# Another written-out order of a fused linear-attention and feed-forward kernel

## The chip, the cores and the metric

The kernel runs on one core of one Trainium2 chip. The metric is the device time of one execution, in microseconds, as the median over runs; lower is better. The core has five engines that each work through their own list of instructions in order: PE (matmul), DVE and ACT (elementwise work), POOL (elementwise work and the issue of DMAs that convert a type on the way) and SP (the issue of other DMAs). They wait for each other by semaphores alone. Matmul results land in PSUM, eight banks of 128 x 512 f32, which DVE and ACT read and POOL does not in this kernel.

## What is computed

```python
def phi(x):                       # q and k scaled by 64 ** -0.25 first
    proj = einsum('bhsd,md->bhsm', x, omega)
    h = proj - sum(x * x, -1) / 2
    return exp(h - max(h, -1)) / sqrt(m)
kv  = einsum('bhsm,bhsd->bhmd', phi(k), v)
z   = sum(phi(k), over s)
num = einsum('bhsm,bhmd->bhsd', phi(q), kv)
den = einsum('bhsm,bhm->bhs', phi(q), z) + 1e-6
x   = (num / den) as 4608 rows of 512      # 8 batches x 576 tokens, 8 heads x 64
h   = x @ w_in                             # 512 x 2048
out = (h * clip(h + 3, 0, 6) / 6) @ w_out  # 2048 x 512
```

All inputs and the output are f32.

## The kernel before

The program first lists its 1963 operations and then emits them. An operation is one call of `op(...)`; it has a number (its place in the listing), a name, the engines that may take it, what it reads and writes, and a function that emits its instructions. The table `ORDER` at the top holds, for each engine, the numbers of the operations in the order in which that engine runs them. `Prog.schedule` walks these lists: the list in which a number stands is the engine that does the operation, and nothing is ever moved past its neighbour. `Prog.emit` then puts a semaphore wait ahead of an instruction where a predecessor runs on another engine. So an instruction that must wait holds up everything behind it in its list. 76 small dummy matmuls ("idle", L576) may be put where the schedule leaves PE empty in the first 21 us; the trace shows 65 of them.

**Stage 1, attention of one batch** (`attention`, `pair`, `burst`; b = 0 to 7). DMAs load k, q and v (`load`, L622): for batch 0 in f32, for later ones k and q through POOL's queue in bf16, and v through SP's. Each of these has main parts (names like v00, v10, k00, k10, q01: 512 tokens of each head) and a leftover (kl, ql0, ql1, vl: the last 64 tokens). k and q are transposed: on PE for batches 0 and 1 (names T), by transposing DMAs on SP after that (Tdmak, Tdmaq, L748). K and Q are matmuls with omega; from batch 3 on both go in four bursts R (L767, L770). ACT takes the exponentials eK and eQ (L786, L795, L818, L835). DVE takes the maxima mx and their reciprocals cc. v is scaled by cc into vc (L939, on POOL in one instruction or on ACT in eight), vcc is its column of cc, vcl the same for leftovers. kv (L957, L959) is the product over tokens, kvz its copy out of PSUM, num (L985) the product with the q side, rec and div the division by the denominator. The result x goes through X, Xdma and Sdma (transposes) to xT, or to xS for the leftover tokens of all batches, which make up a ninth block. The buffer v32 exists once, vl, vc and vcl twice.

**Stage 2, feed-forward of one block of 512 tokens** (`mlp`; block 0 to 8, one block behind the attention). mm1 (L1054; L1199 for block 0, whose weights arrive in four quarters wi0 to wi3, L595, wi0 in two halves) gives the hidden units, relu on ACT and g on DVE (L1060, L1062, L1208, L1210) the activation, in f16. The second product goes by seven block products P.0 to P.6 (L1312) of sums and differences of quarter matrices, a scheme with seven products in place of eight; the sums S1 to S4 of the activations run on POOL (L1240), and on POOL or DVE for the later half of block 8. Results leave PSUM as p1, u2, u3, C11, C21, C22, C12 (L523, L1328) into the one buffer osb, and then by the stores outw (L1408). Block 0 uses a plain product instead, mm2 (L1224), with stores out.0.0 to out.0.3 (L1234). Blocks 7 and 8 use seven products for the first matmul too (`mm1_pair`, mm1a to mm1d, L1133; copies s1, s2, s3; sums a1, a2). The last product of block 8 goes in three parts, P8.60 to P8.62 (L1381), with stores outl (L1392).

**What sets the order around the places that matter below.** w_in's quarters wait for the landing of q11.0 (`W_GATE`) and go through POOL's queue, in POOL's list order. PE's op 431, mm1.0A.12, is the first that needs wi3. vl and v of batch b = 2 wait for a piece of w_out; for b from 3 on they wait for the mm1 of block b - 2 with at = 9, which for vl.3 is mm1.1.12. v00.2 also waits until the vc of batch 1 have read v32. In block 8, P8.3 adds into the PSUM bank that u2.8 reads first.

| numbers | names | engines allowed |
|---|---|---|
| 33, 34, 35, 36, 37 | wi0 (two halves), wi1, wi2, wi3 | POOL |
| 17, 19, 22 to 25, 31, 32 | k00, k01, q00, q10, q01, q11, ql0, ql1 of batch 0 | SP |
| 120, 123, 132, 126, 135, 129, 141 | castk0.10, castk0.11, castq0.0B, .0A, .1B, .1A, .l | POOL, ACT, DVE by part |
| 192, 193, 195, 210, 225, 226, 240, 241 | vcl.0 twice, vc.0.0, vc.0.1, vc.0.2, vcc.0.2, vc.0.3, vcc.0.3 | POOL, ACT |
| 197, 199, 212, 431 | kv.0.0, num.0.0A, kv.0.1, mm1.0A.12 | PE |
| 468, 469, 470, 690 | vl.2, v00.2, v10.2, vl.3 | SP |
| 402, 584, 614 | Sdma.1, out.0.0, out.0.3 | SP |
| 635, 683, 684, 685 | S31.0 (S3 of block 1), k00.3, k10.3, kl.3 | POOL |
| 523, 524, 526, 528 | vcl.2 twice, vc.2.0, kv.2.0 | 528 PE, others POOL or ACT |
| 796, 797 | u2.1, P1.3 | DVE, PE |
| 1806, 1895, 1924 | X2.8, S18.2, S18.3 (S1 of block 8) | POOL, DVE |
| 1921, 1922, 1923, 1799, 1803, 1937 | g1.8.7, S38.3, S28.3, C21.7, C12.7, u2.8 | DVE |
| 1893, 1894, 1931 to 1934 | S38.2, S28.2, S48.0 to S48.3 | POOL, DVE |

Of the kernel before, what the change touches and what calls it, by code (L numbers as in the profile page):

```python
# [20 lines left out]
        13, 118, 139, 156, 124, 144, 150, 162, 115, 168, 147, 127, 153, 121, 159, 165, 136, 130, 133, 177, 185, 175,  # L21
        183, 197, 187, 142, 212, 179, 181, 199, 204, 214, 171, 227, 242, 202, 217, 229, 244, 219, 410, 416, 173, 189,
        417, 232, 404, 254, 247, 405, 222, 234, 406, 207, 249, 407, 257, 411, 412, 418, 413, 419, 422, 280, 425, 252,
        237, 260, 428, 300, 431, 434, 437, 440, 286, 284, 282, 443, 318, 306, 303, 288, 446, 449, 309, 312, 452, 298,
        296, 455, 315, 324, 294, 345, 458, 290, 575, 292, 321, 353, 576, 577, 327, 341, 335, 585, 586, 337, 339, 587,
        595, 588, 596, 331, 605, 366, 333, 578, 329, 579, 597, 355, 589, 590, 379, 598, 591, 368, 371, 592, 392, 580,
        581, 343, 606, 599, 381, 358, 607, 384, 600, 582, 394, 397, 601, 374, 608, 361, 609, 602, 387, 400, 610, 611,
        612, 638, 514, 626, 506, 629, 512, 623, 641, 632, 653, 504, 508, 499, 647, 644, 662, 656, 659, 484, 475, 487,
        496, 478, 481, 674, 668, 520, 518, 490, 493, 677, 510, 516, 671, 784, 785, 528, 502, 794, 533, 540, 530, 787,
        545, 542, 800, 564, 552, 788, 717, 554, 795, 569, 566, 557, 797, 798, 697, 801, 803, 804, 710, 807, 808, 811,  # L30
        817, 826, 724, 820, 737, 814, 832, 841, 829, 835, 739, 742, 749, 844, 847, 850, 761, 862, 856, 859, 773, 754,
        865, 778, 766, 751, 972, 988, 775, 973, 763, 982, 975, 976, 983, 885, 985, 986, 989, 898, 991, 992, 1005, 999,
        1014, 1002, 995, 996, 1017, 905, 1008, 1023, 1020, 1029, 925, 1035, 1032, 912, 1038, 1044, 937, 1050, 927,
        1047, 949, 1053, 939, 942, 930, 1160, 1161, 1176, 954, 961, 1170, 966, 951, 963, 1163, 1171, 1086, 1164, 1173,
        1174, 1073, 1177, 1179, 1180, 1093, 1202, 1193, 1190, 1187, 1183, 1184, 1100, 1205, 1196, 1113, 1208, 1217,
        1211, 1118, 1220, 1223, 1125, 1226, 1115, 1137, 1127, 1235, 1130, 1139, 1238, 1232, 1142, 1149, 1241, 1348,
        1349, 1151, 1364, 1154, 1351, 1274, 1352, 1358, 1359, 1281, 1365, 1361, 1362, 1390, 1375, 1378, 1381, 1367,
        1368, 1393, 1371, 1372, 1384, 1405, 1261, 1399, 1414, 1396, 1420, 1411, 1408, 1426, 1301, 1313, 1429, 1303,
        1318, 1306, 1536, 1315, 1423, 1325, 1537, 1288, 1552, 1539, 1540, 1327, 1546, 1330, 1547, 1462, 1337, 1549,
        1342, 1339, 1550, 1553, 1469, 1555, 1556, 1476, 1559, 1560, 1449, 1563, 1569, 1566, 1572, 1581, 1501, 1593,  # L40
        1506, 1503, 1489, 1584, 1525, 1494, 1578, 1491, 1530, 1527, 1513, 1587, 1518, 1596, 1515, 1599, 1602, 1614,
        1608, 1611, 1617, 1631, 1632, 1662, 1675, 1634, 1665, 1691, 1678, 1667, 1635, 1680, 1704, 1670, 1694, 1641,
        1720, 1696, 1683, 1642, 1707, 1699, 1723, 1709, 1733, 1644, 1645, 1725, 1712, 1749, 1736, 1650, 1738, 1728,
        1762, 1752, 1651, 1741, 1754, 1809, 1765, 1647, 1648, 1812, 1767, 1822, 1757, 1654, 1814, 1655, 1770, 1825,
        1817, 1838, 1827, 1778, 1779, 1841, 1851, 1830, 1843, 1867, 1781, 1854, 1782, 1846, 1856, 1880, 1870, 1788,
        1872, 1859, 1883, 1789, 1885, 1909, 1875, 1794, 1896, 1791, 1792, 1888, 1899, 1795, 1912, 1901, 1941, 1914,
        1797, 1798, 1904, 1917, 1801, 1935, 1925, 1926, 1802, 1936, 1928, 1929, 1938, 1939, 1942, 1960, 1957, 1945,
# [3 lines left out]
        0, 21, 17, 23, 19, 22, 25, 24, 31, 27, 32, 26, 28, 29, 30, 269, 270, 271, 474, 473, 472, 471, 470, 468, 690,  # L51
        469, 402, 614, 584, 694, 696, 594, 693, 695, 692, 604, 536, 548, 560, 572, 691, 573, 881, 878, 810, 883, 879,
        806, 745, 757, 781, 769, 882, 782, 880, 884, 1069, 998, 1072, 1066, 1070, 1071, 994, 1068, 933, 945, 970, 957,
        969, 1067, 1260, 1259, 1257, 1258, 1186, 1133, 1121, 1145, 1157, 1182, 1254, 1158, 1256, 1255, 1374, 1370,
        1447, 1445, 1446, 1448, 1309, 1443, 1333, 1321, 1345, 1444, 1346, 1442, 1509, 1497, 1533, 1521, 1562, 1558,
        1534, 1653, 1657, 1800, 1804, 1953, 1952, 1959, 1962, 1950, 1956,
    ],
    "ACT": [
        18, 20, 117, 119, 157, 145, 151, 163, 132, 169, 148, 129, 154, 193, 166, 196, 160, 178, 211, 184, 137, 176,
        186, 225, 182, 180, 243, 188, 172, 218, 174, 190, 223, 408, 414, 420, 423, 281, 426, 238, 208, 429, 253, 432,  # L60
        301, 435, 438, 441, 283, 285, 444, 261, 319, 307, 304, 447, 310, 450, 313, 289, 299, 352, 297, 325, 346, 316,
        453, 291, 293, 354, 322, 328, 342, 336, 338, 456, 340, 332, 378, 367, 334, 391, 330, 459, 390, 380, 344, 593,
        583, 362, 375, 388, 401, 613, 507, 515, 630, 627, 624, 513, 642, 633, 639, 654, 505, 509, 500, 648, 645, 603,
        663, 657, 660, 476, 497, 482, 479, 485, 675, 488, 494, 519, 669, 491, 523, 511, 672, 517, 503, 529, 539, 678,
        521, 551, 550, 553, 565, 720, 718, 723, 722, 706, 703, 704, 700, 708, 698, 403, 713, 711, 716, 715, 736, 709,
        812, 702, 748, 818, 747, 729, 821, 727, 815, 725, 730, 827, 833, 830, 836, 759, 842, 848, 845, 851, 863, 857,
        774, 860, 866, 974, 977, 897, 894, 891, 896, 892, 888, 886, 899, 890, 903, 921, 901, 1000, 1006, 1003, 923,
        1015, 1018, 906, 936, 904, 1009, 1024, 908, 1021, 911, 1030, 910, 1036, 1033, 913, 574, 915, 1039, 1045, 918,
        938, 1051, 1048, 917, 1054, 959, 960, 962, 1091, 1087, 1092, 1089, 1079, 1084, 1076, 1082, 1074, 1078, 1080,
        1085, 1098, 1099, 1094, 1096, 1194, 1191, 1108, 1203, 1188, 1112, 1111, 1206, 1103, 1197, 1105, 1101, 1209,  # L70
        1212, 1124, 1136, 1218, 1221, 1106, 1224, 1126, 1227, 1138, 1147, 1148, 1239, 1233, 1236, 1242, 1350, 1277,
        1280, 1279, 1275, 1284, 1287, 1282, 1376, 1353, 1379, 1391, 1382, 1286, 1312, 1394, 1385, 1406, 1262, 1270,
        1268, 1266, 1400, 1264, 1415, 1267, 1397, 1297, 1412, 1273, 1409, 1272, 1427, 1324, 1421, 1323, 1430, 1538,
        1424, 1293, 1291, 1289, 1541, 1336, 1294, 1338, 1468, 1465, 1463, 1467, 1474, 1472, 1470, 1159, 1475, 1479,
        1477, 1482, 1481, 1450, 1452, 1458, 1456, 1564, 1455, 1570, 1567, 1454, 1488, 1573, 1502, 1461, 1582, 1460,
        1490, 1585, 1526, 1579, 1514, 1594, 1588, 1597, 1603, 1600, 1609, 1615, 1612, 1618, 1633, 1663, 1664, 1676,
        1677, 1666, 1692, 1679, 1671, 1693, 1636, 1673, 1695, 1684, 1705, 1706, 1686, 1722, 1708, 1700, 1724, 1702,
        1713, 1734, 1735, 1715, 1750, 1737, 1729, 1731, 1753, 1763, 1742, 1764, 1744, 1758, 1810, 1813, 1823, 1760,
        1771, 1824, 1773, 1826, 1818, 1820, 1839, 1831, 1842, 1780, 1852, 1853, 1847, 1833, 1783, 1849, 1860, 1881,
        1882, 1862, 1884, 1876, 1878, 1897, 1889, 1891, 1900, 1913, 1905, 1918, 1907, 1920, 1927, 1930, 1948, 1949,  # L80
        1951,
    ],
    "DVE": [
        16, 12, 11, 15, 14, 5, 138, 4, 9, 140, 10, 125, 7, 158, 146, 116, 191, 152, 164, 6, 122, 128, 149, 155, 194,
        209, 134, 167, 170, 131, 161, 141, 239, 224, 198, 143, 200, 213, 201, 205, 215, 216, 228, 203, 206, 230, 245,
        231, 220, 246, 221, 233, 255, 248, 235, 236, 250, 258, 256, 251, 409, 415, 259, 421, 424, 8, 427, 1623, 430,
        433, 436, 302, 287, 439, 1624, 445, 347, 442, 308, 305, 448, 350, 451, 311, 314, 320, 295, 363, 1625, 454,
# [1414 lines left out]
```

The softmax here doesn't subtract the row's maximum and nothing guards it: scores larger than these inputs give would overflow.

## Time and profile before

| | |
|---|---|
| median of 6 runs | 304.25 us (303.53 to 306.3) |
| the profiled execution, its own time | 306.3 us |
| its span, first to last instruction | 304.5 us |
| PE, DVE, POOL, ACT busy | 97%, 81%, 78%, 70% of the span |
| granted TensorE clock | 1.00 |
| DMA | 44.89 MB moved, mean 147 GB/s |
| chain that ended last, by engine | PE 87%, DMA 7%, POOL 1%, SPq 1%, ACT 1%, issue 1%, DVE 1% |

The profile page is one execution as the hardware profiler saw it. A group is named by line, engine, operation and tiles, as in "PE p L1054"; PEld is the weight load ahead of a matmul, SPq and POOLq the queues of DMA issues. A row of the timeline or the chain begins with start and length in microseconds. The view by stretch gives, for each stretch, its length and then busy time and instruction count for PE, PEld, DVE, ACT and POOL, the granted clock, the DMA share and GB/s. A row of waits names who waited for whom, the total, the number and the longest. Matmuls overlap each other, so their lengths add up to more than the time they take.

### The profile page before, as it was taken

Reading aid. Unit: us, or ns where it says so; the run is one execution under the profiler, and the core shown is the slowest. Engines: PE = TensorE matmul, PEld = TensorE weight load, DVE = VectorE, ACT = ScalarE, POOL = GpSimd, SP = SyncE. Lnnn points to the kernel's source line nnn. Section 1 sums busy time; section 2 is a strip of 40 time slices with the busy share of each in tenths; the row PEclk is TensorE's granted clock in tenths of the full one; section 3 lists DMA queues with packets and bytes.
Section 4 is the critical chain, followed back from the end, with each engine's and each line's share of the span. In section 5 each row is a group of like instructions: output and inputs, shape, how many; then the busy total and the mean of one; then the engine's idle time right before and its main releaser. Section 6 shows DMA issues by size and latency. Waiting matters only on the chain.

```text
span 304.5 us, 7405 instructions
## 1 busy us (share of the span) xinstructions
PE 295.7 (97%) x2795; PEld 210.9 (69%) x2800; DVE 246.6 (81%) x547; ACT 214.2 (70%) x516; POOL 237.4 (78%) x255
## 2 busy tenths in 40 slices
PE   7898999999999999999999999999999999999995
PEld 5677975545677558655875576657756688888884
DVE  4788896859988796679878967688698999999875
ACT  5796898479958982899479954597586677576410
POOL 2783776059796999799969896998958999999990
PEclk9999999999999999999999999999999999999999
DMA  7999998999999898799959958897732500110034
GB/s 238 277 179 190 249 203 84 190 196 118 213 200 167 92 215 230 148 147 222 189 132 119 176 148 226 99 229 136 146 94 41 178 1 2 69 72 2 0 140 139
DMA packets 90100, 44.89 MB, mean 147 GB/s; under 512 B 57936, under 2 KB 87760, under 8 KB 90064
## 3 DMA queue, kind: packets, MB, share of 16 engines
q1 hardware_dynamic: 62496, 31.04, 45.5%
q0 software_dynamic: 26592, 12.46, 33.3%
q10 hardware_dynamic: 976, 0.92, 1.0%
q8 instruction: 22, 0.36, 0.5%
q14 instruction: 14, 0.11, 0.1%
HBM read 36.73 MB, written 9.44 MB: 152 GB/s over the span
## 4 chain that ended last, share of the span: by engine, by line
PE 87%; DMA 7%; POOL 1%; SPq 1%; ACT 1%; issue 1%; DVE 1%
PE p L1312 31%; PE p L1054 26%; PE p L1133 8%; PE p L1224 5%; PE p L1199 3%; DMA wi<-in_moe_w_in_dram 3%; PE p L985 3%; PE p L957 3%; PE p L767 2%; DMA q<-in_q_dram 2%; DMA v<-in_v_dram 2%; PE p L770 2%; SPq L622 1%; PE p L831 1%; POOL vc L941 1%
## 5 line engine op out<-in xcount | busy, mean ns | idle before, releaser
L1054 PE MATMUL p<-xT,wi 128*128 128x512 f16 x384 | 89.9, 379 | 0.1
L1062 DVE SCALAR_TENSOR_TENSOR gT<-tsb,p 128x512 f16<-128x512 f16 x96 | 62.1, 675 | 12.8 <-ACT tsb L1060 12.2
L1060 ACT ACTIVATE tsb<-p 128x512 f16<-128x512 f32 x96 | 55.3, 605 | 14.7 <-PE p L1054 8.9
L1054 PEld LDWEIGHTS p<-xT,wi 128*128 128x128 f16 x384 | 35.8, 98 | 38.5 <-issue 1.1
L1312 PE MATMUL p<-wo,gT 128*128 128x256 f16 x368 | 45.3, 273 | 0.0
L1240 POOL TENSOR_TENSOR gT<-gT 128x512 f16<-128x512 f16 x32 | 37.0, 1155 | 3.2 <-DVE gT L1062 0.9
L1312 PEld LDWEIGHTS p<-wo,gT 128*128 128x128 f16 x368 | 35.0, 98 | 6.4 <-issue 1.1
L1240 POOL TENSOR_TENSOR s<-gT 128x512 f16<-128x512 f16 x31 | 36.2, 1168 | 3.8 <-DVE gT L1062 1.7
L1240 POOL TENSOR_TENSOR s<-gT,s 128x512 f16<-128x512 f16 x31 | 35.9, 1158 | 2.6 <-DVE gT L1062 0.3
L1240 POOL TENSOR_TENSOR gT<-gT,s 128x512 f16<-128x512 f16 x30 | 34.7, 1158 | 2.4
L791 DVE TENSOR_REDUCE mx<-kp 128x4 f32<-128x512 bf16 (+1 forms) x50 | 29.7, 622 | 6.5 <-ACT kp L786 6.4
L795 ACT ACTIVATE qpT<-p 128x512 bf16<-128x512 f32 (+1 forms) x50 | 27.5, 569 | 7.7 <-PE p L770 7.1
L622 POOL DMA_DIRECT2D qb<-in_q_dram x28 | 19.6, 715 | 17.0 <-PE p L1054 15.8
L941 POOL TENSOR_TENSOR vc<-v,cc 128x512 bf16<-128x512 f32 x22 | 23.4, 1064 | 10.9 <-DVE cc L935 4.1
L1312 PE MATMUL p<-t,gT 128*128 128x256 f16 x256 | 31.6, 273 | 0.0
L786 ACT ACTIVATE kp<-p 128x512 bf16<-128x512 f32 (+1 forms) x50 | 26.2, 566 | 7.5 <-PE p L770 7.5
L1001 DVE TENSOR_TENSOR xb<-p,rec 128x256 f16<-128x256 f32 (+1 forms) x64 | 28.4, 470 | 0.3
L1312 PEld LDWEIGHTS p<-t,gT 128*128 128x128 f16 x256 | 24.4, 98 | 4.5 <-issue 1.6
L523 ACT COPY p<-p 128x256 f32<-128x256 f32 (+1 forms) x42 | 16.4, 402 | 14.9 <-PE p L1312 8.6
L1181 ACT ACTIVATE tsb<-p 128x512 f16<-128x512 f32 x32 | 18.7, 601 | 8.3 <-PE p L1133 6.2
L1183 DVE SCALAR_TENSOR_TENSOR gT<-tsb,p 128x512 f16<-128x512 f16 x32 | 21.1, 679 | 0.5 <-ACT tsb L1181 0.3
L943 ACT ACTIVATE vc<-v,cc 128x64 bf16<-128x64 f32 x80 | 20.2, 344 | 0.0
(132 smaller groups left out, 583.1 us busy)
## 6 DMA issues: line engine op xcount, KB each, us to landing
v<-in_v_dram SPq DMA_DIRECT2D x14, 512.0 KB, 5.1
out_dram<-osb SPq DMA_DIRECT2D x14, 512.0 KB, 3.9
kb<-in_k_dram POOLq DMA_DIRECT2D x14, 256.0 KB, 5.3
qb<-in_q_dram POOLq DMA_DIRECT2D x14, 256.0 KB, 5.7
wo<-in_moe_w_out_dram POOLq DMA_DIRECT2D x8, 256.0 KB, 9.2
wi<-in_moe_w_in_dram POOLq DMA_DIRECT2D x3, 512.0 KB, 7.4
q<-in_q_dram SPq DMA_DIRECT2D x4, 256.0 KB, 6.1
v<-in_v_dram SPq DMA_DIRECT2D x4, 256.0 KB, 5.8
```

Of the source, the lines that this page charges most:

```text
L622: lambda E: E.dma_start(dst, src), prio + 0.001 * turn_of[0], reads=gate, writes=keys,
L786: op("ACT", actt(128 * (d1 - d0)), lambda E, lh=lh, ko=ko, part=part: E.activation(ko, out_of(part, 0, lh)[0].rearrange("p (x m) -> p x m" ...
L791: op("DVE", dvet(128 * (d1 - d0)), lambda E, ko=ko, mo=mo: E.reduce_max(mo, ko, axis=AX.X), p0 + 0.01, reads=[("kp", 0, d, lh) for d in ra ...
L795: op("ACT", actt(128 * (d1 - d0)), lambda E, lh=lh, part=part: E.activation(qd[:, part[0]:part[1], lh, :], out_of(part, 1, lh)[0].rearrang ...
L941: return E.tensor_tensor(vcm[:, :, 0:D], v32[:, m, :, :], cbc, ALU.mult)
L1001: op("DVE", dvet(128 * n), lambda E: E.tensor_tensor(xv(i0, i1), psum()[:, :, :, 0:64], rbc, ALU.mult), t + 0.01, reads=[vn, ("rec", ru)], ...
L1054: ins = E.matmul(ring.t[vh.slot], wi[:, c, 128 * f:128 * f + 128], xv[:, c, :], start=(c == 0), stop=(c == NJ - 1))
L1060: op("ACT", actt(512), lambda E: E.activation(tsb[tu][:], ring.t[vh.slot], AF.Relu, bias=0.5, scale=1.0 / 6.0), t - 0.1, reads=[vh], write ...
L1062: op("DVE", dvet(512), lambda E: E.scalar_tensor_tensor(gT[gu][:, f, :], tsb[tu][:], 1.0, ring.t[vh.slot], ALU.min, ALU.mult), t - 0.1, re ...
L1133: ins = E.matmul(dst, w(c), x[:, c, :], start=start and c == 0, stop=c == 1, skip_group_check=True)
L1240: op(engines, {"POOL": 0.07 + n / 455.0, "DVE": 0.1 + n / 850.0}, lambda E: E.tensor_tensor(dst, x, y, ALU.subtract if minus else ALU.add) ...
L1312: ins = E.matmul(ring.t[v.slot][:, 256 * j:256 * j + 256], a[:, f, 128 * j:128 * j + 128], w[:, f, :], start=(first and f == 0 and j == 0) ...
```

## The change

The table `ORDER` alone is changed; no function, shape or buffer is touched. All five lists are written anew, from front to end. The change is described as the same instructions on every engine in another sequence. Read against each other, the lists hold the same 1887 numbers in all, but 73 of them stand in another engine's list than before: SP goes from 115 to 114, ACT from 435 to 445, DVE from 547 to 543, POOL from 251 to 246; PE keeps its 539. Those that move are small copies between ACT and DVE (s1, s2, s3, kvz, Xev, Tev), vcc and vcl between ACT and POOL, four vc (vc.1.3 from ACT to POOL; vc.3.3, vc.6.1, vc.6.3 from POOL to ACT), C11.4 and C11.5 (ACT to DVE), p1.1 and p1.3 (DVE to ACT), casts of batch 0, Swv (ACT or POOL), X2.8, S18.2 and S18.3 from POOL to DVE, and the last stores between SP and ACT.

```diff
--- before.py
+++ after.py
...
-        13, 118, 139, 156, 124, 144, 150, 162, 115, 168, 147, 127, 153, 121, 159, 165, 136, 130, 133, 177, 185, 175,
-        417, 232, 404, 254, 247, 405, 222, 234, 406, 207, 249, 407, 257, 411, 412, 418, 413, 419, 422, 280, 425, 252,
...
+        118, 13, 139, 124, 150, 115, 144, 156, 121, 153, 147, 159, 165, 162, 168, 133, 130, 136, 127, 183, 177, 185,
+        219, 416, 417, 232, 247, 254, 234, 405, 406, 407, 257, 412, 413, 237, 418, 419, 249, 222, 422, 280, 425, 428,
...
-        0, 21, 17, 23, 19, 22, 25, 24, 31, 27, 32, 26, 28, 29, 30, 269, 270, 271, 474, 473, 472, 471, 470, 468, 690,
-        469, 402, 614, 584, 694, 696, 594, 693, 695, 692, 604, 536, 548, 560, 572, 691, 573, 881, 878, 810, 883, 879,
-        806, 745, 757, 781, 769, 882, 782, 880, 884, 1069, 998, 1072, 1066, 1070, 1071, 994, 1068, 933, 945, 970, 957,
-        969, 1067, 1260, 1259, 1257, 1258, 1186, 1133, 1121, 1145, 1157, 1182, 1254, 1158, 1256, 1255, 1374, 1370,
-        1447, 1445, 1446, 1448, 1309, 1443, 1333, 1321, 1345, 1444, 1346, 1442, 1509, 1497, 1533, 1521, 1562, 1558,
-        1534, 1653, 1657, 1800, 1804, 1953, 1952, 1959, 1962, 1950, 1956,
+        0, 21, 17, 19, 22, 23, 25, 24, 31, 32, 28, 26, 27, 30, 29, 269, 271, 270, 473, 474, 472, 471, 470, 690, 584,
+        468, 469, 402, 696, 594, 694, 693, 695, 691, 536, 548, 614, 604, 560, 572, 692, 573, 882, 881, 806, 883, 810,
+        878, 745, 757, 769, 781, 879, 884, 880, 1069, 994, 782, 998, 1066, 1071, 1070, 1072, 1067, 933, 945, 969, 957,
+        1068, 970, 1259, 1257, 1260, 1258, 1133, 1186, 1121, 1145, 1157, 1158, 1182, 1254, 1256, 1255, 1374, 1370,
+        1447, 1445, 1321, 1446, 1448, 1333, 1443, 1442, 1309, 1345, 1346, 1444, 1509, 1497, 1533, 1521, 1534, 1562,
+        1558, 1653, 1657, 1800, 1804, 1948, 1949, 1959, 1950, 1956,
...
+        1913, 1918, 1907, 1920, 1927, 1930, 1952, 1953, 1962, 1951,
...
-        1898, 1887, 1910, 1911, 1793, 1890, 1796, 1902, 1903, 1892, 1915, 1916, 1906, 1919, 1799, 1921, 1908, 1922,
...
+        1902, 1793, 1903, 1796, 1892, 1906, 1915, 1916, 1908, 1919, 1921, 1922, 1923, 1799, 1895, 1803, 1924, 1937,
...
-        1, 2, 123, 114, 120, 126, 35, 135, 3, 33, 192, 34, 195, 210, 36, 226, 240, 241, 264, 262, 37, 263, 266, 265,
-        461, 689, 687, 686, 688, 635, 684, 636, 683, 637, 650, 685, 652, 651, 665, 524, 527, 526, 538, 680, 563, 562,
...
-        1866, 1837, 1865, 1784, 1785, 1836, 1786, 1893, 1894, 1895, 1924, 1931, 1932,
+        1, 2, 3, 114, 132, 34, 135, 141, 35, 33, 192, 196, 195, 210, 36, 226, 240, 264, 262, 37, 263, 266, 265, 268,
...
+        463, 462, 689, 687, 688, 686, 685, 683, 635, 684, 637, 636, 650, 652, 651, 665, 524, 523, 526, 538, 539, 680,
...
+        1786, 1784, 1865, 1893, 1836, 1787, 1894, 1932, 1931,
...
```

## The prediction

> **What bounds the kernel now.** I read the page first. PE stands at 97% busy, but busy time counts overlapping instructions, so I went on to the busy time by stretch of the span, cut where the chain of waits changes its character.
>
> ```profile
> span 304.5 us, 7405 instructions
> ...
> PE 295.7 (97%) x2795; PEld 210.9 (69%) x2800; DVE 246.6 (81%) x547; ACT 214.2 (70%) x516; POOL 237.4 (78%) x255
> ```
>
> ```profile
> 0.00:30.00 30.00, 25.47 (x279) 19.75 (x280) 20.60 (x68) 22.02 (x52) 17.16 (x30) 1.00 1.13 221
> 30.00:80.00 50.00, 49.73 (x391) 31.43 (x397) 40.90 (x82) 40.52 (x92) 29.81 (x37) 1.00 1.11 172
> 80.00:92.00 12.00, 11.32 (x169) 9.40 (x166) 10.19 (x30) 7.80 (x24) 10.90 (x11) 1.00 1.18 232
> 92.00:240.00 148.00, 147.94 (x1395) 95.92 (x1394) 118.76 (x268) 110.73 (x274) 126.13 (x133) 1.00 0.88 155
> 240.00:290.00 50.00, 50.00 (x460) 44.45 (x458) 47.00 (x91) 31.97 (x73) 46.81 (x41) 1.00 0.11 43
> 290.00:301.40 11.40, 11.28 (x112) 9.96 (x109) 8.83 (x14) 1.17 (x2) 6.55 (x6) 1.00 0.34 124
> ```
>
> First number: length; second: PE busy; then PEld, DVE, ACT, POOL; the last two are the granted clock (1.00) and DMA share and rate. From 30 us to PE's end near 301.4, PE lacks 0.27 + 0.68 + 0.06 + 0 + 0.12 = 1.13 us. That is all a resequencing can win there: it removes no matmul. Is PE really saturated while busy? The chain has 88 matmuls of 256 columns in 9.61 us, 0.109 each, where one lasts 0.273; and 16 of 512 columns in 3.45 us, 0.216 each, where one lasts 0.379. They are back to back at their spacing.
>
> The Trainium skill, Perfetto Trace Analysis, section Identifying the Most-Contended Engine, says that matmul busy time is a poor measure and that weight loading should be looked at; by that, 69% would leave much to gain. The spacing decides here, so I do not use it.
>
> Before 30 us the PE waits name the cause, and the chain shows what the wait hangs on:
>
> ```profile
> PE p L1199 <- DMA wi<-in_moe_w_in_dram: 1.2, 1, 1.2
> ...
> PE p L1312 <- DVE u L1328: 0.3, 1, 0.3
> PE p L957 <- POOL vc L941: 0.3, 1, 0.3
> ```
>
> ```profile
> 20.98 8.85 DMA wi<-in_moe_w_in_dram
> 29.96 3.65 PE p L1199 x32
> ...
> 72.78 6.05 DMA v<-in_v_dram
> 78.83 1.42 issue
> 80.25 1.05 POOL vc L941
> 81.35 0.43 PE p L957 x8
> ```
>
> The last quarter of w_in (wi3) sets when PE starts mm1.0A.12 (op 431), and PE had been idle 1.24 us there. The tail, 301.4 to 304.5, is the last output piece. The profiled execution took 306.3 us, 1.8 more than its span, and 2.05 more than the median of the six runs, 304.25. I work out a difference from the profiled execution and add it to 304.25.
>
> **Step 1, the front (0 to 30 us).** Op 431 is PE's 71st operation in both lists, and the 70 ahead of it are the same set. Swaps before it matter only if PE arrives over 1.24 us later, or if wi3 lands at another time. By the new lists, PE's last chain ahead of mm1 (castq0.1A at the landing of q01 near 11.1, the exponentials at 0.48 each, kv.0.0, num.0.0A) comes out a few tenths earlier than before, so wi3 decides.
>
> ```profile
> 10.32 0.95 POOL L595 DMA_DIRECT2D wi<-in_moe_w_in_dram  x1 [0.48 <-DMA q<-in_q_dram]
> ...
> 12.20 0.71 POOL L595 DMA_DIRECT2D wi<-in_moe_w_in_dram  x1
> ...
> 16.61 0.85 POOL L595 DMA_DIRECT2D wi<-in_moe_w_in_dram  x1
> ...
> 20.98 0.76 POOL L595 DMA_DIRECT2D wi<-in_moe_w_in_dram  x1
> ```
>
> POOL no longer does vcc.0.3 (0.23) ahead of wi3, so wi3 is issued about 0.25 earlier. But counted by microsecond, the POOL queue's packets run without a pause from 13.2 us to 31 at 160 to 200 KB per us: an earlier issue into a full queue wins little. The other way: wi0's second half (256 KB) now goes first, at about 10.3, and the 512 KB of wi1 follow only after castq0.1B (0.62) and castq0.l (some 0.35), at about 12.3. In the old order the first packets moved 2.9 us after the first issue. If that delay is all latency, 256 KB at 183 KB/us run dry near 14.6 and wi1 starts near 15.2; a second gap (wi2, issued near 16.8) adds some 0.3. Bounds: -0.25 and +0.9. I take **+0.3**, nearer to the full queue.
>
> **Step 2, batch 2's v (72 to 82 us).** vl.3 waits for mm1.1.12 and goes out at 72.38; v00.2 stands behind it, goes out at 72.78, and lands 7.3 us later (the longest landing in the view of tile v), 80.1. vc.2.0 then starts at 80.25, and PE waits for kv.2.0. New: out.0.0 and vl.2 stand between the two. At their old issue spans (0.43 and 0.53) v00.2 goes out 1.06 later, near 73.85, behind 256 + 128 KB in SP's queue. Against it: kl.3, which POOL issued at 73.38, is now issued before S31.0, near 66. Counted in the trace, its 512 packets of 128 bytes move in 76 to 80 us, among v00.2's. Other 512 KB v loads land 4.3 to 5.4 us after issue. So 73.85 + 5.4 + about 1 for the two in front = 80.2 where the queue is free; the best, 73.85 + 4.3 = 78.2, ends the wait. PE arrives at kv.2.0 about 0.5 before the old start. Bounds: -0.5 (wait gone) and, at the old pace of 512 KB in 4.2 us, 384 KB more = 3.15 later, +3.1. vcl.2's other half goes from ACT (1.07) to POOL (0.62), which still fits ahead of vc.2.0. I take **-0.2**.
>
> The Trainium skill, DMA: Bandwidth & Descriptors, section Queues, rings and completion order, says that a DMA engine takes descriptors of one ring in order and takes turns between rings. By it, v00.2 cannot pass the two transfers, which speaks against this change; the trace's landings of SP's queue near there (vl.3, v00.2, xs, out) do come in order of issue.
>
> **Step 3, P1.3 (89.5 us).** It waits for u2.1 (DVE 0.70) after P1.2. The same three small groups of matmuls (num.2.2B, num.2.3A, num.2.3B) fill that time in the new list, in another order: **0**.
>
> **Step 4, the end.** POOL loses X2.8, S18.2 and S18.3 (1.16 each) to DVE.
>
> ```profile
> 290.20 0.68 DVE L1240 TENSOR_TENSOR s<-gT 128x512 f16<-128x512 f16 x1
> 290.92 1.25 DVE L1240 TENSOR_TENSOR s<-gT,s 128x512 f16<-128x512 f16 x1
> ...
> 295.19 2.10 DVE L1240 TENSOR_TENSOR gT<-gT,s 128x512 f16<-128x512 f16 x2 [1.05 <-PE p L1312]
> ```
>
> On DVE a sum costs 0.68 to 1.25 here. g1.8.7 ends near 289.57 as before; then come S38.3, S28.3, C21.7 (0.69), S18.2, C12.7 (0.69), S18.3, u2.8 (0.69). P8.3 overwrites what u2.8 reads, so PE waits for u2.8 (old: done 294.13, P8.3 at 294.88). Four sums at 0.68: 289.57 + 2.72 + 2.07 = 294.4, no wait. At 1.25: 296.6, 1.7 late. POOL is done with S28.2 by about 291 and then idle, so the two moved sums run beside nothing: 0.68 each, and S28.3 about 1.0: 294.7. I take **+0.2** of 0 to +1.7.
>
> **Step 5, the rest.** 73 operations change engine: vc.3.3, vc.6.1 and vc.6.3 go from POOL (1.05) to ACT (2.03 for the eight), vc.1.3 the other way; small copies swap between ACT and DVE. From 30 to 290 us ACT is 64% to 81% busy by stretch, POOL 60% to 94%. They lie beside PE, and a copy that comes late costs PE only what it is late. PE shows 0.06 us idle in 92 to 240, so there is nothing to win and something to lose: 0 to 3 x 0.98 = +2.9; I take **+0.2**, nearest to the row of idle PE.
>
> Sum: +0.3 - 0.2 + 0 + 0.2 + 0.2 = +0.5: **304.8 us**.
>
> **Rivals.** (a) *Slower by SP's queue*: v00.2 is held up by out.0.0 and vl.2. Each 0.1 that it lands after 79.6 costs PE 0.1; at the upper bound of step 2 the time is 304.25 + 3.1 = 307.4, and over 0.5% is reached at a landing 1.5 later than the old 80.1. For it: the order in SP's list is plain. Against it: kl.3's small packets are gone from those microseconds. (b) *Faster*: both waits of PE at 81 and 89 go, the 1.13 us of idle PE vanish, and wi3 comes with its issue 0.25 earlier: 304.25 - 1.4 = 302.9. Against it: P1.3's wait has the same cause in the new list, and the queue in front of wi3 is full. (c) *Not what it says*: the engines do not keep their instructions (ACT's list grows from 435 to 445, POOL's falls from 251 to 246). If the lengthened ACT chain at the vc's (0.98 each, three times) falls on PE: 304.25 + 2.9 = 307.2. Against it: ACT has idle time there.
>
> **How the numbers follow.** The forecast, within 0.5% (302.7 to 305.8; about what a measurement of this kernel can tell from no change), 0.58. Rival (a) 0.17, (c) and a late DVE at the end together 0.14: slower 0.31. Rival (b) 0.11 for passing its own 302.9 by a wi3 that lands earlier still. The range goes from 303.1, near rival (b), to 307.0, just under (a) and (c).
>
> **What would show it.** Step 1: PE's wait on wi at L1199 and its start, 29.96, within -0.3 to +0.9. Step 2: the landing of v near 80, POOL's vc near 79 to 81, and PE's wait at L957. Step 3: PE's 0.3 on u at L1328 stays. Step 4: a wait at L1312 on DVE near 295. Step 5: PE busy in 92 to 240 still over 147 of 148. I am wrong if 431 starts outside that window, or if PE shows over 1 us of waits in 92 to 290.

## The result and the profile after

The changed kernel takes 307.16 us, median of 19 runs (304.88 to 311.84), against 304.23 us, median of 40 (303.26 to 306.3). The ratio is 1.0083, 95% interval 1.0064 to 1.0101: 2.5 us slower, where the forecast was 0.5. Executions over 1.5% above the fastest of their kernel are left out of this ratio and of those below.

The two profiles hardly differ. First the page of the changed kernel (its own time 306.53), then its busy time by stretch, then PE's waits:

```profile
span 304.7 us, 7406 instructions
...
PE 296.2 (97%) x2795; PEld 211.5 (69%) x2799; DVE 246.0 (81%) x543; ACT 216.9 (71%) x530; POOL 232.1 (76%) x250
```

```profile
0.00:30.00 30.00, 27.06 (x290) 21.28 (x291) 21.80 (x69) 22.21 (x54) 16.23 (x29) 1.00 1.13 224
30.00:80.00 50.00, 49.79 (x399) 31.64 (x402) 40.95 (x82) 39.55 (x86) 33.96 (x41) 1.00 1.13 188
...
92.00:240.00 148.00, 147.88 (x1395) 95.80 (x1394) 119.95 (x266) 112.91 (x290) 122.09 (x129) 1.00 0.87 154
...
290.00:301.40 11.40, 9.91 (x97) 8.43 (x95) 8.62 (x15) 1.17 (x2) 2.75 (x3) 1.00 0.45 160
```

```profile
PE p L1199 <- DMA wi<-in_moe_w_in_dram: 0.5, 1, 0.5
...
PE p L1312 <- DVE u L1328: 0.4, 1, 0.4
```

Read alone, this says "faster": PE does 1.6 us more before 30 us, the wait for wi3 fell from 1.2 to 0.5, the one for kv.2.0 is gone, and DVE's last instruction ends 1.3 us earlier (before, then changed):

```profile
301.32 0.42 DVE L1389 TENSOR_TENSOR osb<-p,u 128x256 f32<-128x256 f32 x1 [0.18 <-PE p L1381]
```

```profile
300.03 0.42 DVE L1389 TENSOR_TENSOR osb<-p,u 128x256 f32<-128x256 f32 x1 [0.18 <-PE p L1381]
```

Yet the span is 0.2 longer. The missing time stands behind the last instruction of PE: the DMA view from the issue of the last store (outl0) to the end, first before, then changed (KB of one issue, then microseconds from issue to landing):

```profile
out_dram<-osb SPq DMA_DIRECT2D x1, 128.0 KB, 2.2
```

```profile
q14 instruction: 1, 0.01, 1.1%
...
out_dram<-osb SPq DMA_DIRECT2D x1, 128.0 KB, 3.7
```

One packet of 8192 bytes on queue 14, which the profile calls "instruction", lies in the store's flight (302.33 us, 0.76 long). The store's last eight packets of 1024 bytes move one after another only from its end, 303.09 us, on; all the others had ended by 302.36. That fits one DMA engine held up by it (the trace does not name a packet's engine). Before, the last such packet came at 299.95, 1.8 us ahead of that store's issue.

Secondly, the profiled execution of before was the slowest of its 40 runs, so its waits need not be typical.

### The profile page after: what moved, and what is told of

Read it like the earlier page. It is cut to its first block, busy times and chain, and to the rows that moved or that the text cites. A ratio compares the mean times of both kernels' runs of the same rounds, so it can differ in the third digit from the quotient of the medians.

```text
span 304.7 us, 7406 instructions
## 1 busy us (share of the span) xinstructions
PE 296.2 (97%) x2795; PEld 211.5 (69%) x2799; DVE 246.0 (81%) x543; ACT 216.9 (71%) x530; POOL 232.1 (76%) x250
## 4 chain that ended last, share of the span: by engine, by line
PE 85%; DMA 5%; ACT 3%; DVE 3%; SPq 1%; issue 1%; POOL 1%; POOLq 0%
PE p L1312 29%; PE p L1054 25%; PE p L1133 8%; PE p L1224 5%; PE p L1199 3%; PE p L985 3%; DMA wi<-in_moe_w_in_dram 3%; PE p L957 2%; PE p L767 2%; DMA q<-in_q_dram 2%; PE p L770 2%; PE p L831 2%; PE p L811 1%; PE p L576 1%; SPq L622 1%
## 5 line engine op out<-in xcount | busy, mean ns | idle before, releaser
L1240 POOL TENSOR_TENSOR gT<-gT 128x512 f16<-128x512 f16 x30 | 35.0, 1166 | 2.8 <-DVE gT L1062 0.7
L941 POOL TENSOR_TENSOR vc<-v,cc 128x512 bf16<-128x512 f32 x20 | 21.8, 1091 | 10.3 <-DVE mx L791 4.7
L523 ACT COPY p<-p 128x256 f32<-128x256 f32 (+1 forms) x46 | 18.4, 411 | 13.7 <-DVE osb L1328 4.1
L943 ACT ACTIVATE vc<-v,cc 128x64 bf16<-128x64 f32 x96 | 24.4, 363 | 1.3 <-DMA v<-in_v_dram 0.6
```

What stands on the lines that cost most here:

```text
L943: ins = E.activation(vcm[:, i, 0:D], v32[:, m, i, :], AF.Copy, scale=cc[pb][:, c0 + i:c0 + i + 1])
L1240: op(engines, {"POOL": 0.07 + n / 455.0, "DVE": 0.1 + n / 850.0}, lambda E: E.tensor_tensor(dst, x, y, ALU.subtract if minus else ALU.add) ...
```

## The experiments

Hybrids take some operations from the changed lists and the others from before's, on every engine. The ratio is to before, on the same chip. PE's idle time is counted here from start to start, less the spacing of the matmul before (0.109 us for 256 columns, 0.216 for 512); the rows of the views count from a matmul's recorded end and show 0.16 less.

**The changed kernel again**, unchanged.

> The changed kernel once more, for a second profile of it. In its first profiled execution PE's op 431 started at 28.63 us (29.96 before) and the last elementwise instruction ended 1.30 us earlier than before, yet the last store landed 3.71 us after its issue began (2.24 before), so that the span came out as before; over all runs the kernel is 2.7 us slower. Theory (tail): the last store is late in most executions, because an 8192-byte instruction-fetch packet stands in front of its last packets. Then this profile shows again DVE's end near 300.4, a last landing over 3 us after the issue, and a fetch packet inside the last 3 us; time 306.9. Rival (the time is lost inside): this profile shows the last DVE instruction at 302 us or later and PE waits of over 2 us in all between 30 and 290 us, which the first profile did not have. Second rival (front): op 431 starts 1 us or more later than 28.63.

Measured: ratio 1.0113 (1.0079 to 1.0146). Landing 3.16 us after the issue, with the packet in it. But DVE ended at 302.6, not at 300.4: op 431 started at 30.32, behind a late first load of k (PE waited 1.8 us for it), and PE was idle 0.62 in front of mm1.3.11. The tail is real and is not alone.

**Front, middle and end alone.**

```diff
 front_only, SP
-        0, 21, 17, 23, 19, 22, 25, 24, 31, 27, 32, 26, 28, 29, 30,
+        0, 21, 17, 19, 22, 23, 25, 24, 31, 32, 28, 26, 27, 30, 29,
...
 middle_only, SP
-        ... 881, 878, 810, 883, 879, 806, 745, 757, 781, 769, 882, 782, 880,
+        ... 882, 881, 806, 883, 810, 878, 745, 757, 769, 781, 879, 884, 880,
...
 end_only, DVE
-        ... 1799, 1921, 1908, 1922, 1923, 1803, 1937,
+        ... 1908, 1919, 1921, 1922, 1923, 1799, 1895, 1803, 1924, 1937,
```

> The order of the changed kernel for the 236 operations that start in the first 31 us, the order of before for the other 1651. Theory (tail): the front gains what PE's op 431 gained in the profile, 1.3 us, and the end is that of before: 303.0 us, ratio 0.996. Rival (front): the transfers of w_in or batch 1 come late in most executions, and the whole 2.5 us is here: 306.8, ratio 1.008. Rival (middle): no more than the front's gain.

> The order of the changed kernel for the 1594 operations between 31 and 285 us alone, with before's front and end. Most of the operations that change engine are here (vc.3.3, vc.6.1 and vc.6.3 on ACT among them). Theory (tail): PE had 0.7 us of idle in this stretch in both kernels, so 304.2, ratio 1.000 within 0.002. Rival (the engines do not hide their work, as the prediction's rival c has it): 306.8 to 307.2, ratio 1.008 to 1.010, with PE waits to match.

> The order of the changed kernel for the last 57 operations alone (from 285 us on: block 8's sums S18 on DVE, its stores, and the swap of four stores between SP and ACT). Theory (tail): this holds the loss; with the front of before, which is 1.3 us later, the time is 304.25 + 2.7 + 1.3 = 308.2 at most, at least 306.5: ratio 1.007 to 1.013, and the last landing comes over 3 us after its issue. Rival (front or middle): ratio 1.000, within 0.003, last landing 2.2 us after its issue.

Measured: front 1.0043 (1.0018 to 1.0069), middle 1.0047 (1.0023 to 1.0071), end 1.0003 (0.9987 to 1.0019). In this form the theory fell: the end's lists do not bring the late store with them (landing 2.2 us after the issue in all three). Front and middle also had a wait that neither kernel has, 0.54 and 0.57 us of idle PE ahead of P8.2; in front_only:

```profile
PE p L1312 <- POOL s L1240: 0.4, 1, 0.4
```

The cut at 285 us had exchanged sums on POOL. So about 0.55 of each loss is the experiment's own.

**The front without the flaw**: changed lists for the first 31 us, before's for the rest to the letter.

> As the first front run, but without its flaw: there the cut at 285 us had also exchanged two sums of block 7 and 8 on POOL (S47.2 ahead of S28.0), which put a wait of 0.54 us in front of P8.2 (286.81 us) that neither kernel has. Here the rest is before's list to the letter. Theory (front and cut): the front itself costs 0.75 us, because wi3 lands 0.9 to 1.5 us later after mm1.0A.0 and POOL's queue moved only 122 KB in the microsecond at 15 us where it moves 195: 304.9, ratio 1.0025, and no wait in front of P8.2. Rival (all of the first run's loss was the front): ratio 1.0043 again, 305.3. Second rival (all of it was the cut and chance): ratio within 1.001.

Measured: 304.24 us, ratio 1.0018 (0.9991 to 1.0044); seven runs at 303.6 to 304.3, five at 305.0 to 307.0. No wait at P8.2. (The 122 KB in the expectation was misread: front_only's queue moves 0.21 MB in the microsecond at 15 us. The pauses are given below.) The interval holds both no loss and the 0.75 us expected.

**DVE's instruction count.** The built programs have 582 instructions on DVE before and 580 after; 584 in front_only and end_only, 576 in middle_only (the traces record four fewer in each). Three kernels move that count and little else; a fourth, after_pool4, is the control.

```diff
 after_dve584
-    op("DVE", 0.1, lambda E: E.memset(om[0:64, 1, :], 0.0), -9, writes=["omz1"])
+    op("DVE", 0.1, lambda E: [E.memset(pad[:, i:i + 1], 0.0) for i in range(4)] and E.memset(om[0:64, 1, :], 0.0), -9, writes=["omz1"])
 after_pool4: the same four memsets ahead of POOL's third operation
 before_dve580: ORDER, two memsets from DVE to POOL
-        1, 2, 123, 114, 120, 126, 35, 135, 3, 33,
+        1, 2, 5, 4, 123, 114, 120, 126, 35, 135, 3, 33,
 after_dve576: ORDER, 4, 5, 7 and 9 from DVE to POOL, behind 2
```

> The changed kernel with four more memsets of one column each on DVE near 4.5 us, where DVE waits for k; nothing else differs. DVE's program is 584 instructions long then, as in the two kernels whose last 8192-byte packet of queue 14 came 1.5 us ahead of the last store (582 in before, 580 in the changed kernel, 576 in the middle run). Theory (fetch in the tail): the packet goes back to 1.5 us ahead of the last store's issue, the last store's wait falls from 3.7 us to 2.2, and the time from 306.9 to 305.7, ratio 1.005. Rival (the packet is harmless, or its place is not DVE's count): the tail stays at 3.5 us or more, ratio 1.008 to 1.010.

> The reverse: the kernel before with two of DVE's first memsets (the zeros of om) on POOL near 1.5 us, so that DVE's program is 580 instructions long as in the changed kernel; every other list is before's. Theory (fetch in the tail): the last 8192-byte packet of queue 14 now comes 1.5 to 2 us after the last store's issue, the last landing comes 3.5 us or more after it, and the time is 304.0 + 1.2 = 305.2, ratio 1.004. Rival: ratio within 1.001, landing 2.2 us after the issue.

> Control for the four memsets: the changed kernel with the same four one-column memsets on POOL near 1.5 us instead of on DVE, so that DVE's program stays at 580 instructions. Theory (fetch in the tail): the last 8192-byte packet of queue 14 still falls into the last store's flight, the span ends 3.6 us or more after the store's issue begins, time 306.9, ratio 1.008 to 1.011. Rival (four small instructions in the first microseconds shift the front favourably, whatever the tail): 304.5, ratio 1.002, as with the memsets on DVE.

> The changed kernel from the other side: four of DVE's first memsets (zeros of om, ones of vl) on POOL near 1.5 us, DVE's program 576 instructions long. Theory: as in the middle run (576), the last packet of queue 14 comes after the last store has landed, the span ends 2.7 us after that store's issue began, time 304.5, ratio 1.002, as with 584. Rival (a shorter program still meets the store, or the gain of 584 was the front's): ratio 1.008 or more.

| kernel | DVE instructions | last q14 packet, from outl0's issue | landing after the issue | ratio to before |
|---|---|---|---|---|
| before | 582 | -1.82 | 2.23 | 1 |
| after | 580 | +1.85 | 3.72 | 1.0083 (1.0064 to 1.0101) |
| after_dve584 | 584 | -2.06 | 2.23 | 1.0017 (0.9992 to 1.0042) |
| after_pool4 | 580 | +1.54 | 3.32 | 1.0065 (1.0040 to 1.0090) |
| after_dve576 | 576 | +4.50 | 2.23 | 1.0057 (1.0031 to 1.0083) |
| before_dve580 | 580 | +1.56 | 3.09 | 1.0021 (1.0004 to 1.0038) |

The same DMA view, from outl0's issue to the end, of after_dve584 and then of before_dve580:

```profile
out_dram<-osb SPq DMA_DIRECT2D x1, 128.0 KB, 2.2
```

```profile
q14 instruction: 1, 0.01, 0.8%
...
out_dram<-osb SPq DMA_DIRECT2D x1, 128.0 KB, 3.1
```

Four small instructions on DVE move the packet; the same four on POOL do not; two fewer on DVE bring it into the store's flight in the kernel before. Over all 14 profiles the five with 580 have it in the store's flight and land 3.09 to 3.72 us after the issue, the nine others 2.22 to 2.24: a cost of 0.9 to 1.5 us, 1.1 in the mean. So it is shown that DVE's instruction count places the packet and that the packet in the flight delays the landing. As for times, after_pool4 (306.5 us) and before_dve580 (305.0; its landing 3.09, not 3.5) came near what was expected, after_dve584 fell below it (304.5, not 305.7), and after_dve576 stayed at 306.2, not 304.5, although its landing is on time. Something else is lost inside.

**The wait ahead of mm1.3.11.** In after_dve584, ACT's timeline and then PE's row (start, length, and in brackets the idle time ahead with what ended it):

```profile
126.33 0.61 ACT L1060 ACTIVATE tsb<-p 128x512 f16<-128x512 f32 x1
128.15 2.02 ACT L943 ACTIVATE vc<-v,cc 128x64 bf16<-128x64 f32 x8 [1.21 <-DMA v<-in_v_dram]
130.07 0.57 ACT L786 ACTIVATE kp<-p 128x512 bf16<-128x512 f32 x1
```

```profile
130.70 1.47 PE L1054 MATMUL p<-xT,wi 128*128 128x512 f16 x6 [0.49 <-ACT kp L786]
```

ACT stands 1.21 us before vc.4.0 for a load of v, then works 2.02 us, and only then reads the bank that PE wants for mm1.3.11. vc.4.0 needs both loads of v; the one that ends the wait is v10.4, landing at 128.12. SP's timeline tells why it is late: after_dve584 first, then before.

```profile
114.62 6.63 SPq L1030 DMA_TRANSPOSE xT<-xb  x4
121.30 0.58 SPq L622 DMA_DIRECT2D v<-in_v_dram  x1
...
123.20 0.58 SPq L622 DMA_DIRECT2D v<-in_v_dram  x1
```

```profile
112.43 0.53 SPq L622 DMA_DIRECT2D v<-in_v_dram  x1
...
113.56 8.26 SPq L1030 DMA_TRANSPOSE xT<-xb  x4
...
124.52 0.58 SPq L622 DMA_DIRECT2D v<-in_v_dram  x1
```

Before, v00.4 goes out ahead of the four Xdma.3 and v10.4 alone behind them. In the changed list both stand behind, 1.9 us apart, and v10.4 takes 4.8 to 5.2 us to land instead of 4.2 to 4.5. It lands 99.1 to 100.2 us after op 431's start with the changed lists throughout, 97.9 to 98.8 where before's list stands there. But ACT's list changed too: before's has vc.4.0 further back, behind the relu numbered 1003, and starts it 1.7 to 2.2 us after that landing. PE's idle time at mm1.3.11 was 0.07 to 1.15 us in seven profiles with the changed lists throughout (once at mm1.3.3; mean 0.59), 0.97 in middle_only, none in rest_clean584 (below), where v10.4 landed earliest against R4.0, and none with before's list.

```diff
 after_vc4_later, ACT
-        ... 1000, 923, 906, 911, 1003,
+        ... 1000, 906, 911, 923, 1003,
```

> The changed kernel with one number moved on ACT: vc.4.0 (923, eight instructions, 2.03 us) now stands behind eK4.10.0 and eQ4.10.1 (906, 911) instead of ahead of them. In the changed kernel and in the middle run vc.4.0 starts 0.02 to 0.03 us after the landing of v00.4, and PE's mm1.3.11 waits for the bank that eK4.10.0 reads: 0.40, 0.62 and 0.97 us in three profiles. Theory (a late v on ACT holds PE): this wait goes in every execution, 306.9 - 0.7 = 306.2, ratio 1.007. Rival (the middle's loss lies elsewhere): the wait moves to kv.4.0 or to the next relu, ratio unchanged at 1.009 within 0.001.

Measured: ratio 1.0083 (1.0052 to 1.0115), as without the move. (In the first profile of the changed kernel PE's idle time there is 0.08, not 0.40, and the landing meant is v10.4's.) The wait at mm1.3.11 is gone and another stands at mm1.3.3, 0.89 us of idle PE; the rival was right:

```profile
PE p L1054 <- DVE gT L1062: 0.7, 1, 0.7
```

ACT's rows of this run:

```profile
130.90 2.01 ACT L943 ACTIVATE vc<-v,cc 128x64 bf16<-128x64 f32 x8
132.80 1.06 ACT L1060 ACTIVATE tsb<-p 128x512 f16<-128x512 f32 x2
```

vc.4.0 no longer waits for v (v10.4 landed at 129.69), but its 2.01 us now hold up the relus behind it instead of the exponential. So the late load is not the whole cause; the place in ACT's list counts as well. Neither vc.4.0 behind the relu 1003, as before has it, nor v00.4 ahead of the transposes was run with the changed lists; which of the two costs PE its time stays open.

**The front's share.**

> Before's front (all operations of the first 31 us, its lists to the letter) and the changed kernel's lists for all the rest, with six one-column memsets on DVE near 4.7 us that make its program 584 instructions long. Theory: the front costs the changed kernel about 0.5 us in the mean, the rest without the tail 0 to 0.3: 304.2, ratio 1.000 within 0.002; this is also the version that could beat before if the changed middle is the better one. Rival (the middle costs 0.8 as the first middle run, less its cut, said): 305.0, ratio 1.0026.

> The changed kernel with the four memsets on DVE (584) and before's order of SP's first 15 loads: q10.0 ahead of k01.0, and v00.0 ahead of ql1.0. In four of six profiles with the changed front PE waited for k (0.3 to 1.8 us) because one of the first transfers was late. Theory (front by SP): these waits go, wi3's gate q11.0 lands 0.25 earlier, and the time falls from 304.5 to 304.1, ratio 1.000, with fewer executions over 306. Rival (the front's loss is POOL's order of w_in, or chance): ratio 1.002 as with 584 alone.

Measured: before's front with the changed rest and 584 instructions 304.3 us, 1.0006 (0.9982 to 1.0031); the changed kernel with 584 and before's SP order for the first loads 306.25 us, 1.0070 (1.0040 to 1.0101). The first takes the loss away, and beats nothing; its profile happens to lack the wait at mm1.3.11. The second came out above its theory and its rival, and speaks against SP's order of the first loads as the front's cause. The extremes of op 431's start, in a before front (end_only) and in a changed one (front_clean):

```profile
27.39 3.66 PE L1199 MATMUL p<-xT,wi 128*128 128x256 f16 x32
```

```profile
30.52 2.67 PE L1199 MATMUL p<-xT,wi 128*128 128x256 f16 x23 [1.60 <-DMA wi<-in_moe_w_in_dram]
```

Two effects are mixed in this pair. In 6 of 13 profiles (after584_sp left out, its front being neither) one of the first loads lands 0.7 to 1.4 us late: q10.0 with before's front (2 of 5), k00.0 with the changed one (4 of 8). Without that, op 431 starts at 27.39, 27.76 and 28.54 with before's front and at 27.89, 28.48, 28.63 and 29.24 with the changed one; with it, at 28.91 and 29.96 against 29.91 to 30.52. Either way the changed front is 0.7 later in the mean. In the four changed fronts with the late load POOL's queue moves 120 to 132 KB in the microsecond from 14 us and 81 to 113 in that from 19, in the nine other profiles 183 to 204 and 168 to 204. That is the gap behind wi0's half that step 1 described, but only behind a late load. In the four changed fronts without one there is no such gap, and yet wi3 is issued at 20.33 to 20.44, against 19.82 to 20.25 in the three of before's, and lands at 27.5 to 29.1, against 26.6 to 28.4; why, stays open. The clean front's interval holds both 0 and 0.7 us, so this share rests on the profiles alone.

## Why the prediction was right in its range and wrong in its sum

By the ratio the time is 304.25 x 1.0083 = 306.8 us, inside the range of 303.1 to 307.0 and near its top. That is luck: the top came from rivals (a) and (c), and neither a late v00.2 nor the three vc that went to ACT made the time. The forecast itself, within 0.5%, did not come, and by its own sign (op 431 outside the window) the prediction was wrong. The step that failed most is the tail, which the sum carried over unchanged.

**The base.** The sum was made on a profiled execution 2.05 us over the median, and its waits were taken as typical. There the first load of q10.0 landed at 7.61 us, where 6.72 to 7.04 is usual, and everything behind it came late. In four other profiles with before's front PE's idle time ahead of op 431 was 0, 0, 0.47 and 0.71, where this one has 1.41, and ahead of kv.2.0, in four others with before's lists around it, 0 to 0.14, not 0.50. There was less to win than "1.13 us of idle PE", and step 1 began from a start of 431 that is not the usual one.

**Step 1** took +0.3 within -0.25 and +0.9. In the changed profile 431 started at 28.63, 1.33 earlier, outside the window named; that compared a late execution with a normal one. Like against like it is +0.7: the direction was right, the size short by 0.4. The gap was seen only behind a late first load, and wi3 was issued 0.3 later in the mean (without the late load), not 0.25 earlier. The queue was also not quite as full as read: 141 KB in the microsecond from 22 us.

**Step 2** took -0.2. Right: v00.2 landed at 77.7, vc.2.0 started at 77.9, and PE has no wait at kv.2.0. The transfers ahead of v00.2 did not make it late (the four landed in order of issue, at 73.4, 75.1, 76.3 and 77.7), and kl.3 was gone: before, 512 packets of 128 bytes move between v00.2's issue and landing, in the changed kernel none. Rival (a), v late by SP's queue, had part of the right mechanism at the wrong batch: batch 4's two loads, behind four transposes, were in the diff's SP list and not looked at.

**Step 3** was right: PE's wait on u at L1328 stays, 0.4.

**Step 4** took +0.2. P8.3 does not wait. S38.3 and S28.3 took 1.37 and 1.26 on DVE, not 0.68 and 1.0, the moved sums S18.2 and S18.3 0.41 each, not 0.68. What is late is p1.8 on ACT, and PE is idle 0.25 us ahead of P8.1 for it. p1.8 waits for DVE's C21.7, which the new list puts behind S38.3 and S28.3:

```profile
288.00 1.37 DVE L1240 TENSOR_TENSOR s<-gT 128x512 f16<-128x512 f16 x1
289.41 1.26 DVE L1240 TENSOR_TENSOR s<-gT,s 128x512 f16<-128x512 f16 x1
...
291.30 0.59 ACT L523 COPY p<-p 128x512 f32<-128x512 f32 x1 [4.05 <-DVE osb L1328]
```

So a late DVE did cost about the +0.2, at another place than named. The end alone measured 1.0003, with 0.16 idle there.

**Step 5** took +0.2 of 0 to +2.9. It measured 0.6 in the mean, around vc.4.0 on ACT. Rival (c)'s time, 307.2, was near; a vc on ACT did hold PE up, but one that was on ACT in both kernels: vc.3.3, vc.6.1 and vc.6.3 brought PE at most 0.05 us more.

**The missing term** is the largest: "the tail, 301.4 to 304.5, is the last output piece" was carried over unchanged, and it cost 1.1 in the mean. The row that could have warned was on both pages: 14 instruction packets on queue 14, the last 1.8 us ahead of the last store's issue in before. With 73 operations moved between engines, the counts of instructions change and with them the packets' places.

Sum by the runs: tail 1.1 + front 0.7 + vc.4.0 0.6 + P8.1 0.25 = 2.65, against 2.5 measured. The spans agree with the terms vc.4.0 and P8.1 taken together, 0.85: between op 431's start and the last matmul's lie 270.56, 270.56 and 271.05 us with before's lists (before_dve580, front_clean, before), and 270.88 to 272.06 in the eight profiles with the changed lists there, 0.75 more in the mean.

The tail is shown by experiment: against the changed kernel's 1.0083, the three versions without the packet in the tail (after_dve584, after_dve576, after584_sp) are 2.0, 0.8 and 0.4 us faster, 1.1 in the mean. The rest is read from profiles, one execution of each kernel, and no time confirms it: rest_clean584, which has the changed lists behind the front, measured 0.2 us over before (-0.5 to 0.9), where 0.85 would be its share. What separates the three versions (1.0017, 1.0057, 1.0070), beyond the late first load, stays open.

## What to carry to other kernels

Before a sum is made on one profile, set its execution against the other runs: where it is the slowest of them, its waits are not the kernel's. Where a change moves instructions between engines, look where each kernel's instruction packets fall against the last store; a few small instructions more or less on one engine can be worth as much as the order of all the others. In a queue in order, read for every moved load what now stands ahead of it, in all batches and not only where the profile shows a wait.

## What the runs showed of the hardware

- Queue 14 carries packets of 8192 bytes; in all 14 profiles the last one's place follows the number of DVE's instructions, whatever ACT has (with 580 it is the same at 614 and at 603 recorded ACT instructions): -1.8 to -2.1 us from the last store's issue with 584, -1.8 with 582, +1.5 to +1.8 with 580, +4.5 to +4.8 with 576. The Trainium skill, Runtime: NRT & Kernel Launch, section Instruction fetch mechanics, says that instructions are refilled in blocks of 16 KiB and that the cost of a boundary is mostly hidden. Here packets of 16384 bytes are seen on queue 8 and of 8192 on queue 14, and in the flight of the last store one costs 0.9 to 1.5 us; the measurement decides.
- Single packets of the first loads can be very slow: one of 1024 bytes took 1.63 us in front_clean (median 0.05), and a load of k landed 1.1 us late with all loads behind it.
- A 128x512 f16 sum on DVE took 0.41 us while POOL was idle and 0.60 to 1.37 beside a sum on POOL (block 8, before and changed). No run here separates this from the other operands.
